# Four operand buffers for the heads of sequences 0 and 1; the last eight weight slots and the output operands change place

## The chip, the core and the metric

The kernel runs on one core of a Trainium2 chip. The metric is the device time of one execution in microseconds (us). Times below are medians of several executions; the views of the profile come from one execution that was taken by the hardware profiler.

TensorE (PE) does the matmuls, with its weight loads (PEld) beside them; VectorE (DVE), ScalarE (ACT) and GpSimd (POOL) do elementwise work; SyncE's queue (SP) starts the transfers (DMA). Each works through its own instructions in program order, and waits where an operand or a buffer is not yet there.

## What is computed

Retention attention with a fixed decay per head, then two feed-forward layers, all in 32-bit floats:

```python
gamma = 1.0 - 2.0 ** (-5.0 - np.arange(H))                   # B, H, S, D = 8, 8, 576, 64
Dmat = np.where(rel >= 0, gamma ** rel, 0.0)                 # rel = pos[:, None] - pos[None, :]
attn = np.matmul(scores * Dmat, v)                           # scores = q k^T / 8
x = attn.transpose(0, 2, 1, 3).reshape(4608, 512)
h = np.maximum(np.maximum(x @ w1, x @ w2), x @ w3)           # 512 -> 768
x = h @ w_out                                                # 768 -> 512
h = x @ w_in                                                 # 512 -> 2048
out = (h * np.clip(h + 3.0, 0.0, 6.0) / 6.0) @ w_out         # 2048 -> 512
```

## The kernel before

**The work and its pieces.** A unit is one pair of heads of one sequence: four units for each of the eight sequences, numbered 0 to 31. Its operands (queries, keys and values of both heads in several layouts) fill one buffer of 128 partitions x 3392 floats, which two transfers of 560 KB load (`load_raw`, L221 from `in_hi` and L224 from `in_lo`), after POOL has zeroed two corners of it (L217, L218). Sequences 0 and 1 (units 0 to 7, class `Summed`) are done at the start by a quicker route than the rest:

- `prepare`: eight multiplications of the keys on ACT (L364);
- `keys_mm`: 16 score matmuls (L268) and 16 wide matmuls (L374) on PE, where each of the wide ones needs one of the eight multiplications;
- `keys_rest`: mask (L289) and growth factors (L386) on DVE;
- `values_mm`: the ninth chunk's scores (L268) and 16 value matmuls (L310) on PE;
- `values_rest`, `last_mm`, `last_rest`: one more mask (L289) and the decay (L314) on DVE, the two last value matmuls on PE, the split of the result into a high and a low part (L55 on ACT, L56 on DVE) for `x`, the operand of the first layer, and for `xe`, which keeps the 64 tokens left over of each sequence. `xe` has one buffer; a transfer (`xed`, L355) empties it after each sequence.

**What runs between the units.** From unit 4 on, two blocks of the first layer follow each unit (`block`, 12 matmuls each of 128x512, L438 to L440; the eight blocks of `early`). The weights of that layer come as 64-bit words, 24 tiles in all. `wa.step` turns one tile at a time into two 32-bit parts: two integer operations on DVE (L116, L117), two on ACT (L119, L122), two more on DVE (L127, L129), one on POOL (L131); then a cast on ACT (L109) and the low part on POOL (L135). A step also starts the load of another tile (`ws`, L97, three buffers). A block's result is copied by ACT (L453) or joined by DVE (L455), and every third one is split into `h` (L55, L56).

**Buffers of units 0 to 7.** Two buffers `raw` and, for units 2 and 3 alone, two buffers in the pool `rooms`. After unit 3 the pool is released, and the pool `moe` (`t`, `h`, `y` of the first layer) takes its place, each of its tiles waiting for what it overlays. Units 4 to 7 have the two `raw` buffers: units 4 and 5 are loaded when units 0 and 1 are done, unit 6 when unit 4 is done, unit 7 when unit 5 is done. Every engine's order is the order in which the program is written (a manual schedule). The loop over the units is, in short:

```python
            if i < HP and i + 2 < HP + 2:       # units 2 to 5
                us[i + 2].prepare()
                us[i + 2].keys_mm()
...
            if i >= HP:
                load_raw(i + 2)
                wa.step()
                flush()
                block(*early.pop(0))
                if i + 2 < len(us):             # units 6 and 7
                    us[i + 2].prepare()
                    us[i + 2].keys_mm()
```

So the keys of units 2 to 5 stand between the values and the last matmuls of the unit two before, those of units 6 and 7 behind its second block. `flush` issues the low parts and transfers that were put off (`late`).

**After the units.** The rest of sequences 0 and 1's first layer runs from a written plan, with weight steps between. Then each sequence's four units run between the blocks of the one before, and the second layer's weights are turned into their parts alongside. From about the middle of the span the second layer runs in 48 groups (6 parts of the tokens x 8) of 7 products of 128x384 each and the projections to the output; each group writes four split operands by `gated` (L55, L56).

**The slots.** Of the 24 weight tiles the first 16 lie in slots `w`, the last 8 in slots `v`, both in the pool `w_pool`. When the first layer is done, the `w` slots take the output weights, and the eight `v` slots (128 x 1024 floats each) take `gated`'s operands and the output rows of `store`.

## Time and profile before

| | |
|---|---|
| time, median of 3 executions | 1555.34 us (1551.84 to 1555.36) |
| time of the profiled execution | 1550.61 us |
| its span, first to last instruction | 1548.8 us |
| TensorE busy | 1491.1 us, 96% of the span |
| VectorE busy | 903.1 us, 58% |
| ScalarE, GpSimd busy | 445.7 us, 29%; 175.6 us, 11% |
| mean granted TensorE clock | 0.989 of full speed |

The profiled execution took 4.7 us less than the median of the others. Its busy times add up over stages with different limits, so the table only says where to look: TensorE is idle for 58 us in all, and the question is in which stage, and on whom it waits there.

### The profile page before, as it was taken

The numbers are of one execution on the slowest core, as the hardware profiler recorded it, in microseconds if no ns is written. First come the engines' busy times: TensorE is split into PE (matmuls) and PEld (weight loads), VectorE is DVE, ScalarE is ACT, GpSimd is POOL, SyncE is SP. The second block draws the span as 40 slices with busy tenths as digits, with TensorE's granted clock in tenths as the row PEclk, the third lists the DMA queues.
The fourth block names the chain that finished last, engine by engine and source line by source line (L and its number), as shares of the span: only waits on it lengthen the run. The fifth ranks groups of instructions, "written<-read, shape, count | busy, mean of one in ns | idle before, by whom it ended". The sixth has DMA issues, their size and how long they took to land.

```text
span 1548.8 us, 24614 instructions
## 1 busy us (share of the span) xinstructions
PE 1491.1 (96%) x9664; PEld 1261.8 (81%) x9664; DVE 903.1 (58%) x1951; ACT 445.7 (29%) x878; POOL 175.6 (11%) x196
## 2 busy tenths in 40 slices
PE   6779999999999999799999999999999999999998
PEld 4557877888888888688888889888898888888887
DVE  4777666867676767512444655655655556565453
ACT  3434322332333233311222222222222223223221
POOL 1335400222222222300000000000000000000000
PEclk9989999999999999899999999999999999999999
DMA  9544135556565655405464435426336445444431
GB/s 217 143 124 124 67 88 136 152 170 173 186 157 167 181 183 145 177 41 197 136 218 116 121 128 184 118 88 226 115 89 230 118 115 196 121 114 132 146 102 41
DMA packets 94659, 220.01 MB, mean 142 GB/s; under 512 B 18320, under 2 KB 21648, under 8 KB 90448
## 3 DMA queue, kind: packets, MB, share of 16 engines
q1 hardware_dynamic: 94544, 218.44, 47.5%
q8 instruction: 77, 1.26, 0.3%
q14 instruction: 38, 0.31, 0.1%
HBM read 174.36 MB, written 44.04 MB: 141 GB/s over the span
## 4 chain that ended last, share of the span: by engine, by line
PE 52%; DVE 4%; ACT 1%; issue 0%; ACTq 0%
PE mm L438 9%; PE mm L440 9%; PE mm L439 9%; PE o L730 5%; PE o L731 5%; PE o L729 5%; PE p L730 2%; PE p L729 2%; PE p L731 2%; DVE g L688 1%; PE o L438 1%; PE o L440 1%; PE o L439 1%; DVE v L56 1%; DVE cc L695 1%; DVE g L687 1%
## 5 line engine op out<-in xcount | busy, mean ns | idle before, releaser
L55 ACT CAST v<-g 128x384 fp32r<-128x384 f32 x192 | 98.6, 513 | 364.5 <-DVE g L688 354.2
L438 PE MATMUL mm<-x,w 128*128 128x512 f32 x468 | 189.2, 404 | 11.7 <-ACT t L453 11.4
L695 DVE TENSOR_TENSOR cc<-mm,c 128x384 f32<-128x384 f32 x144 | 79.8, 554 | 197.0 <-ACT c L700 187.4
L439 PE MATMUL mm<-x,w 128*128 128x512 f32 x468 | 184.8, 395 | 0.0
L440 PE MATMUL mm<-x,w 128*128 128x512 f32 x468 | 184.3, 394 | 0.0
L56 DVE TENSOR_TENSOR v<-g,v 128x384 fp32r<-128x384 f32 x192 | 107.3, 559 | 112.3 <-ACT v L55 111.7
L455 DVE TENSOR_TENSOR t<-mm,t 128x512 f32<-128x512 f32 x108 | 74.3, 688 | 156.4 <-PE mm L440 150.4
L730 PE MATMUL o<-w,v 128*128 128x512 f32 x384 | 151.1, 393 | 0.0
L731 PE MATMUL o<-w,v 128*128 128x512 f32 x384 | 151.0, 393 | 0.0
L729 PE MATMUL o<-w,v 128*128 128x512 f32 x384 | 150.6, 392 | 0.0
L438 PE MATMUL mm<-T,wq 128*128 128x384 f32 x384 | 130.6, 340 | 2.5 <-ACT c L700 1.6
L440 PE MATMUL mm<-T,wq 128*128 128x384 f32 x384 | 129.5, 337 | 0.0
L439 PE MATMUL mm<-T,wq 128*128 128x384 f32 x384 | 129.2, 337 | 0.0
L700 ACT COPY c<-mm 128x384 f32<-128x384 f32 x144 | 68.7, 477 | 178.4 <-PE mm L440 178.4
L131 POOL TENSOR_TENSOR wf<-wf,wp 128x512 f32<-128x512 f32 x56 | 77.5, 1384 | 354.6 <-DVE wp L129 333.7
L438 PEld LDWEIGHTS mm<-x,w 128*128 128x128 f32 x468 | 89.0, 190 | 33.0 <-ACT t L453 12.2
L440 PEld LDWEIGHTS mm<-x,w 128*128 128x128 f32 x468 | 89.3, 191 | 19.3
L439 PEld LDWEIGHTS mm<-x,w 128*128 128x128 f32 x468 | 89.2, 191 | 17.4
L438 PE MATMUL mm<-B,wq 128*128 128x384 f32 x288 | 97.8, 340 | 2.1 <-DVE g L688 1.9
L440 PE MATMUL mm<-B,wq 128*128 128x384 f32 x288 | 97.0, 337 | 0.0
L439 PE MATMUL mm<-B,wq 128*128 128x384 f32 x288 | 96.9, 336 | 0.0
L289 DVE TENSOR_TENSOR raw<-at,mask_sb 64x256 f32<-64x256 f32 (+2 forms) x156 | 56.6, 363 | 54.9 <-PE at L268 35.6
(129 smaller groups left out, 2950.0 us busy)
## 6 DMA issues: line engine op xcount, KB each, us to landing
wq<-wqd SPq DMA_DIRECT2D x336, 256.0 KB, 2.8
ws<-in_w_b SPq DMA_DIRECT2D x32, 512.0 KB, 7.5
raw<-in_hi SPq DMA_DIRECT2D x29, 560.0 KB, 5.7
raw<-in_lo SPq DMA_DIRECT2D x29, 560.0 KB, 7.9
ws<-in_w_a SPq DMA_DIRECT2D x24, 512.0 KB, 3.6
wqd<-y SPq DMA_DIRECT2D x24, 512.0 KB, 2.8
x2d<-y SPq DMA_DIRECT2D x18, 512.0 KB, 3.5
wod<-y SPq DMA_DIRECT2D x16, 512.0 KB, 3.1
```

Source lines behind the costliest of these rows:

```text
L55: nc.scalar.copy(hi, full)
L56: late.append(lambda: (eng or nc.vector).tensor_tensor(out=lo, in0=full, in1=f32(hi), op=ALU.subtract))
L131: nc.gpsimd.tensor_tensor(out=frac, in0=frac, in1=f32(power), op=ALU.mult)
L438: nc.tensor.matmul(ps, lhsT=wh, rhs=xh, start=first, stop=False, skip_group_check=read)
L439: nc.tensor.matmul(ps, lhsT=wh, rhs=xl, start=False, stop=False, skip_group_check=read)
L440: nc.tensor.matmul(ps, lhsT=wl, rhs=xh, start=False, stop=last, skip_group_check=read)
L455: nc.vector.tensor_tensor(out=tmp[t, f], in0=ps, in1=tmp[t, f], op=ALU.max)
L695: nc.vector.tensor_tensor(out=c, in0=a, in1=b, op=ALU.add)
L700: nc.scalar.copy(c, ps)
L729: nc.tensor.matmul(outs[s], lhsT=gh, rhs=wo[f][:, 0, :], start=start, stop=False)
L730: nc.tensor.matmul(outs[s], lhsT=gh, rhs=wo[f][:, 1, :], start=False, stop=False)
L731: nc.tensor.matmul(outs[s], lhsT=gl, rhs=wo[f][:, 0, :], start=False, stop=stop)
```

## The change

- The pool `moe` is allocated first, at the bottom of what was shared space; `rooms` lies above it and lives until unit 7 is done. Its two buffers are of one kind (`room`) now and serve units 2 and 3 and then units 6 and 7.
- `load_raw(i + 4)` follows every unit i up to 5: a unit is loaded when the unit four before it is done. Units 8 and 9 (the first of sequence 2) go into the `raw` buffers of units 4 and 5.
- The keys of all units from 2 to 7 stand between the values and the last matmuls of the unit two before.
- The `flush` after unit 3 is gone; what was put off there is issued at unit 4, behind its first weight step.
- After unit 7 `rooms` is released, and the eight slots `v` are allocated in its place (pool `v_pool`).
- `gated`'s operands and `store`'s rows get eight buffers of their own, `gp`, 128 x 768 floats, in the pool `m2` of the second layer.

```diff
@@ -64,6 +64,7 @@
     wq_d = [dram.tile([P, 7, 2, 2 * P], F32, name=f"wqd{j}") for j in range(F2 // 2)]
     wo_d = [dram.tile([P, 2, 512], F32, name=f"wod{f}") for f in range(F2)]
 
+    moe = tc.alloc_tile_pool(name="moe", bufs=1)
     rooms = tc.alloc_tile_pool(name="rooms", bufs=1)
     at = tc.alloc_tile_pool(name="at", bufs=1, side="right")
     ps_mm = ctx.enter_context(tc.tile_pool(name="ps_mm", bufs=2, space=PSUM))
@@ -138,7 +139,7 @@
         return w_pool.tile([P, 2, 512], F32R, tag="w", bufs=F2, name="w")
 
     def v_tile():
-        return w_pool.tile([P, 2, 512], F32R, tag="v", bufs=NA - F2, name="v")
+        return v_pool.tile([P, 2, 512], F32R, tag="v", bufs=NA - F2, name="v")
 
     def pair():
         return moe.tile([P, 2, 512], F32R, tag="hy", bufs=7, name="y")
@@ -237,6 +238,9 @@
         upper(VS1, Z0)
         lower(KN, HI)
         lower(VS0, RAW)
+
+    def room():
+        return rooms.tile([P, RAW], F32, tag="room", bufs=2, name="room")
 
     def decay(i):
         if i < len(units):
@@ -492,8 +496,8 @@
         nc.sync.dma_start(out=mask_sb[:, 1:], in_=mask[:, 1:])
         nc.sync.dma_start(out=qdec_sb, in_=qdec)
         wa.fetch(1)
-        load_raw(2, rooms.tile([P, RAW], F32, name="room2"))
-        load_raw(3, rooms.tile([P, RAW], F32, name="room3"))
+        load_raw(2, room())
+        load_raw(3, room())
         nc.vector.memset(rebias, -896.0)
         nc.scalar.mul(rebias, rebias, 2.0 ** 23)
         xs[0], xs[1] = x_tile(), x_tile()
@@ -525,7 +529,7 @@
             flush()
             if i >= HP:
                 block(*early.pop(0))
-            if i < HP and i + 2 < HP + 2:
+            if i + 2 < len(us):
                 us[i + 2].prepare()
                 us[i + 2].keys_mm()
             u.values_rest()
@@ -533,21 +537,15 @@
             if i + 1 < len(us):
                 us[i + 1].keys_rest()
             u.last_rest()
-            if i < 2:
-                load_raw(i + HP)
+            if i < HP + 2:
+                load_raw(i + HP, room() if i in (2, 3) else None)
             if i >= HP:
-                load_raw(i + 2)
                 wa.step()
                 flush()
                 block(*early.pop(0))
-                if i + 2 < len(us):
-                    us[i + 2].prepare()
-                    us[i + 2].keys_mm()
-            if i == HP - 1:
-                flush()
-                rooms.release()
-                moe = tc.alloc_tile_pool(name="moe", bufs=1, reuse_waits="tile")
         flush()
+        rooms.release()
+        v_pool = tc.alloc_tile_pool(name="v", bufs=1, reuse_waits="tile")
 
 
         plan = [(1, 0, j) for j in range(3)] + [(0, 0), (0, 2, 2)] + [(1, 1, j) for j in range(3)] + [(0, 1)]
@@ -681,12 +679,15 @@
         flush()
         todo = []
 
+        def g_tile():
+            return m2.tile([P, 2, TH], F32R, tag="gp", bufs=8, name="gp")
+
         def gated(full, s0, f):
 
             g = m2.tile([P, TH], F32, tag="g", bufs=2, name="g")
             nc.vector.tensor_scalar(out=g, in0=full, scalar1=3.0, scalar2=0.0, op0=ALU.add, op1=ALU.max)
             nc.vector.scalar_tensor_tensor(out=g, in0=g, scalar=6.0, in1=full, op0=ALU.min, op1=ALU.mult)
-            parts = v_tile()[:, :, :TH]
+            parts = g_tile()
             split(g, parts[:, 0], parts[:, 1])
             return [(s0 + s, parts[:, :, s * P:(s + 1) * P], f) for s in range(TH // P)]
 
@@ -708,7 +709,7 @@
             return [(slice(C * i, C * (i + 1)), out[(2 * s + i) * S + TB:(2 * s + i + 1) * S, :]) for i in range(2)]
 
         def store(p, s, ps):
-            ob = f32(v_tile()).rearrange("p a n -> p (a n)")[:, :DM]
+            ob = f32(g_tile()).rearrange("p a n -> p (a n)")[:, :DM]
             if s % 2:
                 nc.vector.tensor_scalar(out=ob, in0=ps, scalar1=1.0 / 6.0, scalar2=None, op0=ALU.mult)
             else:
@@ -752,6 +753,7 @@
                 times(Y, 1, "B21", True, True)
                 down(TT - 1, F1 - 1)
                 flush()
+                v_pool.release()
                 moe.release()
                 x_pool.release()
                 m2 = ctx.enter_context(tc.tile_pool(name="m2", bufs=1, reuse_waits="tile"))
```

Line numbers of the kernel after the change are up to 4 higher. Three places in the orders of the engines, before and after.

TensorE, unit 6's keys, before: the end of unit 4's second block (its last matmul stands first), then the keys of unit 6 (`raw`), then unit 5's ninth scores and its values.

```order
L440 MATMUL mm<-x,w 128x512
L268 MATMUL o_166<-raw 64x64 x16
L374 MATMUL o_167<-raw 64x512 x2
L374 MATMUL o_167<-raw 64x448 x2
L374 MATMUL o_167<-raw 64x384 x2
L374 MATMUL o_167<-raw 64x320 x2
L374 MATMUL o_167<-raw 64x256 x2
L374 MATMUL o_167<-raw 64x192 x2
L374 MATMUL o_167<-raw 64x128 x2
L374 MATMUL o_167<-raw 64x64 x2
L268 MATMUL o_164<-raw 64x64 x2
L310 MATMUL o_165<-raw 64x64 x16
```

After the change: the end of unit 4's first block, then the keys of unit 6 (now in `room`), then the two last value matmuls of unit 4.

```order
L444 MATMUL mm<-x,w 128x512
L272 MATMUL o_169<-room 64x64 x16
L378 MATMUL o_170<-room 64x512 x2
L378 MATMUL o_170<-room 64x448 x2
L378 MATMUL o_170<-room 64x384 x2
L378 MATMUL o_170<-room 64x320 x2
L378 MATMUL o_170<-room 64x256 x2
L378 MATMUL o_170<-room 64x192 x2
L378 MATMUL o_170<-room 64x128 x2
L378 MATMUL o_170<-room 64x64 x2
L314 MATMUL at_123<-raw 64x64 x2
```

The 32 matmuls moved ahead of unit 4's last matmuls and of one block. Unit 7's moved in the same way, from behind unit 5's second block to behind its first.

ScalarE at the same place, before: the copy of unit 4's first block, the split of unit 3's or 4's results (`x`, `xe`), a weight step, the eight multiplications for unit 6, and the next weight step's cast.

```order
L453 COPY t<-mm 128x512
L55 CAST x<-yr 128x512
L55 CAST xe<-yr 128x64
L109 CAST w<-wf 128x512
L119 ACTIVATE wp<-wp,rebias 128x512
L122 ACTIVATE wf<-wf 128x512
L364 ACTIVATE raw<-raw,kdec_sb 128x64 x8
L109 CAST w<-wf 128x512
```

After:

```order
L457 COPY t<-mm 128x512
L368 ACTIVATE room<-room,kdec_sb 128x64 x8
L55 CAST x<-yr 128x512
L55 CAST xe<-yr 128x64
L110 CAST w<-wf 128x512
L120 ACTIVATE wp<-wp,rebias 128x512
L123 ACTIVATE wf<-wf 128x512
L110 CAST w<-wf 128x512
```

The eight multiplications moved from behind a split and a weight step to right behind the copy. Unit 7's moved in the same way and now stand right behind the cast of the first `h`.

SyncE's queue from the load of unit 5 on, before (`xed` is the store of sequence 0's `xe`, the pair of `raw` behind it is unit 6, the next pair unit 7, the last row unit 8).

```order
L221 DMA raw<-in_hi 64x2240
L224 DMA raw<-in_lo 64x2240
L97 DMA ws<-in_w_a 128x512 x2
L355 DMA xed<-xe 1024x1x64
L97 DMA ws<-in_w_a 128x512
L221 DMA raw<-in_hi 64x2240
L224 DMA raw<-in_lo 64x2240
L97 DMA ws<-in_w_a 128x512 x2
L221 DMA raw<-in_hi 64x2240
L224 DMA raw<-in_lo 64x2240
L97 DMA ws<-in_w_a 128x512 x2
L221 DMA raw<-in_hi 64x2240
```

After: the two pairs of `room` are units 6 and 7, the pairs of `raw` behind them units 8 and 9.

```order
L222 DMA raw<-in_hi 64x2240
L225 DMA raw<-in_lo 64x2240
L98 DMA ws<-in_w_a 128x512
L222 DMA room<-in_hi 64x2240
L225 DMA room<-in_lo 64x2240
L98 DMA ws<-in_w_a 128x512
L222 DMA room<-in_hi 64x2240
L225 DMA room<-in_lo 64x2240
L98 DMA ws<-in_w_a 128x512
L359 DMA xed<-xe 1024x1x64
L222 DMA raw<-in_hi 64x2240
L225 DMA raw<-in_lo 64x2240
```

Unit 6's load moved ahead of a weight load, `xed` and another weight load; unit 7's ahead of `xed` and three weight loads. Each pair still waits for POOL's two corner writes, and these for the last reader of the buffer's earlier unit.

## Rows read from the trace of the kernel before

**Rows 1.** The page: span, and busy time of each engine.

```profile
span 1548.8 us, 24614 instructions
...
PE 1491.1 (96%) x9664; PEld 1261.8 (81%) x9664; DVE 903.1 (58%) x1951; ACT 445.7 (29%) x878; POOL 175.6 (11%) x196
```

**Rows 2.** Stretches: length; busy PE, PEld, DVE, ACT, POOL; clock; DMA share; GB/s.

```profile
60.00:80.00 20.00, 13.19 (x122) 8.82 (x121) 8.95 (x16) 5.79 (x16) 5.82 (x7) 0.83 0.49 128
...
1000.00:1200.00 200.00, 199.59 (x989) 178.76 (x988) 111.08 (x209) 53.10 (x105) 0.00 (x0) 1.00 0.47 148
```

**Rows 3.** TensorE's timeline, units 4 to 7; idle time and its releaser in brackets.

```profile
65.81 0.47 PE L268 MATMUL o<-raw 64*64 64x64 f32 x2 [3.53 <-DMA raw<-in_hi]
...
68.94 1.65 PE L268 MATMUL o<-raw 64*64 64x64 f32 x25 [2.66 <-DMA raw<-in_lo]
...
75.25 1.15 PE L310 MATMUL o<-raw 128*64 128x64 f32 x32
...
80.64 0.34 PE L310 MATMUL o<-raw 128*64 128x64 f32 x4 [1.27 <-DVE raw L289]
...
86.76 0.47 PE L268 MATMUL at<-raw 64*64 64x64 f32 x2 [2.82 <-DMA raw<-in_hi]
...
89.50 1.65 PE L268 MATMUL at<-raw 64*64 64x64 f32 x25 [2.27 <-DMA raw<-in_lo]
...
101.22 0.34 PE L310 MATMUL o<-raw 128*64 128x64 f32 x4 [1.32 <-DVE raw L289]
...
112.68 0.34 PE L310 MATMUL at<-raw 128*64 128x64 f32 x4 [3.71 <-DVE raw L289]
```

**Rows 4.** The same timeline, the keys of unit 3.

```profile
32.35 1.15 PE L268 MATMUL mm<-room 64*64 64x64 f32 x32
...
33.58 4.10 PE L374 MATMUL mm<-room 64*64 64x512 f32 x32
```

**Rows 5.** SyncE's queue: issue of transfers.

```profile
41.16 8.18 SPq L97 DMA_DIRECT2D ws<-in_w_a  x2
...
59.42 0.49 SPq L221 DMA_DIRECT2D raw<-in_hi  x1
...
59.96 0.59 SPq L224 DMA_DIRECT2D raw<-in_lo  x1
```

**Rows 6.** TensorE's timeline: last matmuls of units 2, 3 and 4.

```profile
45.52 0.34 PE L310 MATMUL o<-room 128*64 128x64 f32 x4
...
53.37 0.34 PE L310 MATMUL mm<-room 128*64 128x64 f32 x4
...
59.00 0.34 PE L310 MATMUL at<-raw 128*64 128x64 f32 x4
```

**Rows 7.** Transfers of the first 130 us: count, size, median us to landing.

```profile
room<-in_lo SPq DMA_DIRECT2D x2, 560.0 KB, 15.0
```

**Rows 8.** ScalarE's timeline: cast of the first h; keys of unit 7.

```profile
80.14 0.62 ACT L55 CAST h<-t 128x512 fp32r<-128x512 f32 x1 [7.50 <-DVE t L455]
...
89.54 2.03 ACT L364 ACTIVATE raw<-raw,kdec_sb 128x64 f32<-128x64 f32 x8 [2.84 <-DMA raw<-in_lo]
```

**Rows 9.** Unit 4's values to unit 7's last matmuls, columns as in rows 2.

```profile
54.97:112.68 57.71, 40.02 (x365) 28.27 (x365) 37.70 (x69) 21.27 (x49) 18.55 (x19) 0.88 0.49 120
```

**Rows 10.** VectorE's timeline: a block's joining, first operation of two weight steps.

```profile
61.69 0.41 DVE L116 TENSOR_SCALAR wp<-ws 128x512 uint32<-128x512 uint32 x1
...
79.41 0.69 DVE L455 TENSOR_TENSOR t<-mm,t 128x512 f32<-128x512 f32 x1 [11.00 <-PE mm L440]
...
88.52 1.47 DVE L116 TENSOR_SCALAR wp<-ws 128x512 uint32<-128x512 uint32 x1
```

**Rows 11.** VectorE's groups in the stretch of rows 9: count, busy us, mean ns.

```profile
L116 DVE TENSOR_SCALAR wp<-ws 128x512 uint32<-128x512 uint32 x7 | 4.9, 704 | 0.0
```

**Rows 12.** TensorE's timeline behind the units.

```profile
149.33 0.50 PE L438 MATMUL mm<-x,w 128*128 128x512 f32 x1 [1.87 <-ACT t L453]
```

**Rows 13.** The page's groups: the cast of the second layer's operands.

```profile
L55 ACT CAST v<-g 128x384 fp32r<-128x384 f32 x192 | 98.6, 513 | 364.5 <-DVE g L688 354.2
```

## The prediction

> **What bounds the kernel now.** I read the page first: TensorE is busy for 1491.1 us of the 1548.8 us span [rows 1], so 58 us are to be had from its waits and nothing from a faster side engine elsewhere. Then the stretches: from 1000 to 1200 us TensorE is busy for 199.59 of 200 us, from 60 to 80 us for 13.19 of 20 at a granted clock of 0.83 [rows 2]. So I went to TensorE's own timeline of the units, and there read what ended each pause. From unit 4's values to unit 7's last matmuls the stretch lasts 57.71 us, of which TensorE works 40.02 [rows 9]. Seven pauses make up nearly all of the rest [rows 3]: four in which the keys of unit 6 (3.53 and 2.66 us) and of unit 7 (2.82 and 2.27 us) wait for the two halves of their operands, and three in which the last value matmuls of units 5, 6 and 7 (1.27, 1.32, 3.71 us) wait for VectorE's mask. The reader should see two things: the transfers are late because they are issued late (unit 6's at 59.42 and 59.96, just behind unit 4's last matmuls at 59.00 [rows 5, 6]), not because the queue is full; and behind each load pause the clock has fallen.
>
> **What the change removes.** First, the four load waits: 3.53 + 2.66 + 2.82 + 2.27 = 11.28 us, if the loads are there in time. Unit 6's operands now go into unit 2's buffer. Its last matmuls end at 45.52 + 0.34 = 45.9 us [rows 6]; POOL's corner writes and the issue take some 0.5 us, so the two halves start at about 46.4 and 46.9. The weight load ahead of them in the queue went out at 41.16, the one now behind them at 49.0 (the last of the two that the row merges [rows 5]), so the queue stands still for nothing. Unit 6's halves took 65.81 - 59.42 = 6.4 us and 68.94 - 59.96 = 9.0 us from issue to the matmul that they released [rows 3, 5]. That puts the later half at about 55.9. The keys come right behind unit 4's first block, at 59.0 [rows 6]: 3 us to spare. Unit 7's buffer is free at 53.7 [rows 6], its halves are there by 63 at the same 9 us, and its keys cannot come before those of unit 6 end at 64.3, with two blocks still between: no wait.
>
> Second, the cold clock. From the second pause on, unit 6's keys take 75.25 - 68.94 = 6.31 us and unit 7's begin with the same row of 1.65 us, so I take as much for them [rows 3]; the same 32 matmuls of unit 3, at full clock, take 33.58 + 4.10 - 32.35 = 5.33 us [rows 4], or 5.2 without the two that ran before the second pause. That is 1.1 us each, 2.2 together, and goes with the waits, since TensorE would now come to these keys from an unbroken block.
>
> Third, 1.27 us before unit 5's last matmuls. They will stand behind unit 7's keys, 5.3 us of work that VectorE can use to finish its mask. This work hides it; without unit 7's keys there the 1.27 us would be back.
>
> Removed in all: 11.28 + 2.2 + 1.27 = 14.75 us.
>
> **What it adds.** No instruction is added but for order. (a) Unit 7's eight multiplications now stand behind ScalarE's cast of the first `h`, and that waits for VectorE's joining of the block which TensorE has just finished. Before, joining plus cast took from 79.41 to 80.76 [rows 8, 10], and the first multiplication of eight takes 2.03 / 8 = 0.25 us [rows 8]: 1.6 us after the block the first wide matmul may start, while the 16 score matmuls ahead of it cover only 1.15 [rows 4]. A pause of 0.5 us if VectorE is free at the block's end. VectorE is then in its second weight step of the pair; by its backlog up to 0.7 us more. I take 0.8, with 0.4 and 1.2 as ends. Unit 6's multiplications stand behind a mere copy, 0.6 us, under the scores: nothing. (b) Unit 4's last matmuls now come one key block later. VectorE waits there for TensorE, and its order goes on with the mask of the next unit only afterwards; since VectorE is busy for 37.70 of 57.71 us [rows 9], it has 20 us of idle time in this stretch, of which 14 go. Some 6 us remain, so VectorE nearly becomes the bound, and the waits of 1.32 and 3.71 us, which are VectorE's own backlog, stay as they are. (c) The store of sequence 0's `xe` goes out later by one weight step's four VectorE operations; the cast of unit 4's `xe` needs it, and comes later itself by a whole key block, 5.3 us: hidden. (d) The block of memory now called `gp` has as many buffers as `v` had, and the same order of casts; the first layer's last weights wait for units 6 and 7, done long before. Nothing, hidden by ScalarE's 364.5 us of idle time before these casts [rows 13].
>
> Sum: 14.75 - 0.8 = 14 us, with ends of 13.5 and 14.4 by (a) alone. VectorE's backlog at the third wait may be up to 1.2 us more or less, so 12 to 16 us. From the profiled 1550.6 us this gives 1536.6; the executions of the median lie 4.7 us higher, so I forecast **1541 us**, and 1539 to 1543 for this case. What follows the units keeps its order and starts, as before, from the point at which TensorE waits for VectorE; the later pause of 1.87 us at 149.33 [rows 12] moves with it.
>
> **Rivals.** (1) VectorE takes over as the bound. The first operation of a weight step took 0.41 us at 61.69 and 1.47 at 88.52 [rows 10], the longer one beside a POOL operation; the seven of the stretch come to 4.9 us [rows 11]. In a denser stretch more of them could fall on POOL's work. If all did, 7 x 1.47 - 4.9 = 5.4 us more on VectorE, which with 6 us of idle time left and its waits for TensorE between would pass almost whole to the end: a gain of about 9, so 1546 us. For it speaks that VectorE is the releaser of three of the seven pauses; against it, that the steps keep their place behind POOL's work of the step before. The Trainium skill, "SBUF — State Buffer", section "Who interferes with whom", says that VectorE and GpSimd share a port pair under an exclusive lock, where the loser waits for the whole instruction; by that rule these operations are blocked, not slowed, and the case is this rival's.
>
> (2) Unit 6's load is late. The first two `room` loads took 15.0 us in the median [rows 7], in a full queue. Then the lower half would land at 61.9, TensorE would wait 2.9 us and lose 1.1 to the clock: a gain of 10, 1545 us. Against it: from 60 to 80 us the transfers' share is 0.49 [rows 2], and 46 to 55 us carries just one more weight load.
>
> (3) The change does not do what it says: POOL or the queue holds the new loads until the next weight step is done, and the keys wait as before in another place. Then only the 1.27 us and a part of the first pause go, within 4 us: 1552 us. Against it stand the queue's issue times above.
>
> (4) Slower. The second layer's operands lie in a new place. If ScalarE's casts into `gp` (513 ns each [rows 13]) or VectorE's low parts were slower there and TensorE waited for them, each of the 48 groups would have to lose more than 14 / 48 = 0.29 us to undo the gain, and 0.39 us to be slower by 0.3%: 1560 us. Against it: shapes, counts and order are the same, and TensorE's pauses there sum to 0.41 us in 200 [rows 2].
>
> **Chances.** Forecast (12 to 16 us): 0.60. VectorE as the bound: 0.17. Late load: 0.08. A larger gain, up to 20 us, where VectorE's backlog shrinks too: 0.03. No effect, or the gain lost later: 0.08. Slower: 0.04. A measurement of this kernel tells 0.3%, 4.7 us, from no change. So faster 0.88, same 0.08, slower 0.04. The range reaches from the larger gain to the two middle rivals with the executions' spread on top: 1536 to 1548 us.
>
> **What would show it.** Right: no pause of TensorE released by a transfer behind 30 us; keys of units 6 and 7 in 5.2 to 5.4 us each; a granted clock near 1 from 56 to 90 us; unit 6's two loads issued at 46 to 47 us; a pause before unit 7's wide matmuls of 0.4 to 1.2 us, released by ScalarE; waits of about 1.3 and 3.7 us for VectorE's mask before the last matmuls of units 6 and 7, and these last ones at about 98 to 99 us instead of 112.68. Wrong: a transfer still named there; unit 7's last matmuls earlier by 14 us but the end by less, which would put the loss behind the units; or TensorE's share in the second layer below that of before.

## The result, and the profile after

The kernel after the change takes 1538.56 us (median of 4 executions, 1535.74 to 1541.06), the kernel before, run beside it on the same chip, 1554.7 us. The ratio is 0.9899, 95% interval 0.9877 to 0.9921: faster by 16 us by the medians, with a forecast of 1541 and a range of 1536 to 1548. The profiled execution of after took 1537.66 us, 12.95 less than that of before. A later run of the same kernel gave 0.9912 [0.9899, 0.9925], 1538.31 us, 14.0 less than the kernel before beside it (1552.28).

The page after, span and busy times, beside [rows 1]:

```profile
span 1535.9 us, 24616 instructions
PE 1489.1 (97%) x9664; PEld 1260.6 (82%) x9664; DVE 904.3 (59%) x1951; ACT 445.9 (29%) x878; POOL 176.0 (11%) x196
```

TensorE's work is the same 9664 instructions. Of the 12.9 us by which the span is shorter, 10.9 are idle time of TensorE (57.7 us before, 46.8 after) and 2.0 are busy time. TensorE's timeline after, in the stretch of [rows 3] (start, length, the instruction, and in brackets idle time and its releaser; lines are up to 4 higher than before):

```profile
54.83 1.15 PE L314 MATMUL at<-raw 128*64 128x64 f32 x32 [1.00 <-DVE yr L318]
...
58.86 1.15 PE L272 MATMUL o<-room 64*64 64x64 f32 x32
...
63.88 0.34 PE L314 MATMUL at<-raw 128*64 128x64 f32 x4
...
71.40 1.15 PE L272 MATMUL at<-room 64*64 64x64 f32 x32
73.15 4.10 PE L378 MATMUL at<-room 64*64 64x512 f32 x32 [0.61 <-ACT room L368]
77.18 0.34 PE L314 MATMUL o<-raw 128*64 128x64 f32 x4
...
86.21 0.34 PE L314 MATMUL o<-room 128*64 128x64 f32 x4 [1.45 <-DVE room L293]
...
97.66 0.48 PE L314 MATMUL at<-room 128*64 128x64 f32 x4 [3.79 <-DVE room L293]
```

The reader should see what is gone from [rows 3]: no pause names a transfer any more, and unit 5's last matmuls (77.18) no longer wait. One pause is new, 0.61 us for ScalarE, and two waits for VectorE's mask are left as they were. Unit 7's last matmuls come at 97.66 us instead of 112.68.

SyncE's queue after, and the landing of unit 6's two halves (last number: median us from issue to landing):

```profile
45.87 0.47 SPq L222 DMA_DIRECT2D room<-in_hi  x1
46.38 0.59 SPq L225 DMA_DIRECT2D room<-in_lo  x1
48.87 0.33 SPq L98 DMA_DIRECT2D ws<-in_w_a  x1
...
58.55 0.60 SPq L359 DMA_DIRECT2D xed<-xe  x1
```

```profile
room<-in_hi SPq DMA_DIRECT2D x1, 560.0 KB, 5.5
room<-in_lo SPq DMA_DIRECT2D x1, 560.0 KB, 7.7
```

The later half is there at 46.38 + 7.7 = 54.1 us, 4.8 us before the keys that read it begin at 58.86. Before, the two halves went out at 59.42 and 59.96 [rows 5].

The stretch from unit 4's values to unit 7's last matmuls after, and the 16 us behind it (columns as in [rows 2]):

```profile
54.83:97.66 42.83, 36.96 (x364) 26.64 (x365) 38.98 (x69) 21.40 (x49) 18.98 (x17) 0.99 0.62 162
...
97.66:113.66 16.00, 16.00 (x61) 12.95 (x62) 9.83 (x16) 6.47 (x12) 6.47 (x6) 0.81 0.31 88
```

The same 16 us before:

```profile
112.68:128.68 16.00, 16.00 (x66) 13.08 (x67) 10.99 (x17) 6.79 (x13) 7.88 (x8) 0.89 0.72 186
```

57.71 us [rows 9] have become 42.83: 14.88 us gained where the change was made. Directly behind, TensorE gets through 61 matmuls in the 16 us in which it did 66 before, at a granted clock of 0.81 instead of 0.89. Unit 7's last matmuls and the four blocks behind them take 125.54 - 112.68 = 12.86 us before and 111.75 - 97.66 = 14.09 after: 1.2 us given back. From unit 7's last matmuls to the end of the span it is 1548.8 - 112.68 = 1436.1 us before, 1535.9 - 97.66 = 1438.2 after, and 1536.2 - 100.14 = 1436.1 in the second run of after. That run has the clock of 0.81 behind the units too, and is level with before at the end all the same. So the 1.2 us repeat, but that the whole time loses anything behind the units is not shown.

### The profile page after: what moved, and what is told of

It reads as the page before. It is cut to its first block, busy times and chain, and to the rows that moved or that the text cites. A ratio compares the mean times of both kernels' runs of the same rounds, so it can differ in the third digit from the quotient of the medians.

```text
span 1535.9 us, 24616 instructions
## 1 busy us (share of the span) xinstructions
PE 1489.1 (97%) x9664; PEld 1260.6 (82%) x9664; DVE 904.3 (59%) x1951; ACT 445.9 (29%) x878; POOL 176.0 (11%) x196
## 3 DMA queue, kind: packets, MB, share of 16 engines
q8 instruction: 77, 1.26, 0.3%
## 4 chain that ended last, share of the span: by engine, by line
PE 52%; DVE 4%; ACT 1%; issue 0%; ACTq 0%
PE mm L442 9%; PE mm L444 9%; PE mm L443 9%; PE o L731 5%; PE o L732 5%; PE o L730 5%; PE p L731 2%; PE p L730 2%; PE p L732 2%; DVE g L689 1%; PE o L442 1%; PE o L443 1%; PE o L444 1%; DVE cc L696 1%; DVE g L688 1%; ACT gp L55 1%
## 5 line engine op out<-in xcount | busy, mean ns | idle before, releaser
L55 ACT CAST gp<-g 128x384 fp32r<-128x384 f32 x192 | 98.5, 513 | 364.9 <-DVE g L689 356.2
L56 DVE TENSOR_TENSOR gp<-g,gp 128x384 fp32r<-128x384 f32 x192 | 107.2, 559 | 112.3 <-ACT gp L55 111.8
L731 PE MATMUL o<-w,gp 128*128 128x512 f32 x384 | 151.1, 393 | 0.0
L732 PE MATMUL o<-w,gp 128*128 128x512 f32 x384 | 151.0, 393 | 0.0
L730 PE MATMUL o<-w,gp 128*128 128x512 f32 x384 | 150.6, 392 | 0.0
L132 POOL TENSOR_TENSOR wf<-wf,wp 128x512 f32<-128x512 f32 x56 | 77.3, 1380 | 346.8 <-DVE wp L130 325.8
L293 DVE TENSOR_TENSOR raw<-at,mask_sb 64x64 f32<-64x64 f32 (+2 forms) x152 | 54.8, 361 | 55.6 <-PE at L272 35.4
```

Of the source, the lines that this page charges most:

```text
L55: nc.scalar.copy(hi, full)
L56: late.append(lambda: (eng or nc.vector).tensor_tensor(out=lo, in0=full, in1=f32(hi), op=ALU.subtract))
L132: nc.gpsimd.tensor_tensor(out=frac, in0=frac, in1=f32(power), op=ALU.mult)
L730: nc.tensor.matmul(outs[s], lhsT=gh, rhs=wo[f][:, 0, :], start=start, stop=False)
L731: nc.tensor.matmul(outs[s], lhsT=gh, rhs=wo[f][:, 1, :], start=False, stop=False)
L732: nc.tensor.matmul(outs[s], lhsT=gl, rhs=wo[f][:, 0, :], start=False, stop=stop)
```

## Experiments

For each kernel "stretch" is the time from unit 4's values to unit 7's last matmuls, the view that tells most: 57.71 us before, 42.83 after, and 42.84 (57.30 to 100.14) in the second run of after. The start of the stretch varies by some us, in part with the first loads, and from its end to that of the span the profiled executions below take 1435.3 to 1439.7 us, so whole times are worse evidence than the stretch. Ratios are to the kernel before, run beside on the same chip.

**1. After once more** (no edit).

> The changed kernel once more, on the same chip as the three kernels below, as their yardstick. Every theory: 12 to 17 us under the kernel before, ratio about 0.990; unit 7's last matmuls at 97 to 99 us.

0.9912 [0.9899, 0.9925], 1538.31 us, with the same stretch to 0.01 us: the measure by which the others are read.

**2. The loads alone.** After the change, but units 6 and 7's multiplications and keys back behind the second block:

```diff
-            if i + 2 < len(us):
+            if i < HP and i + 2 < HP + 2:
                 us[i + 2].prepare()
                 us[i + 2].keys_mm()
...
                 block(*early.pop(0))
+                if i + 2 < len(us):
+                    us[i + 2].prepare()
+                    us[i + 2].keys_mm()
```

> Four buffers and loads four units ahead as in the changed kernel, but the keys of units 6 and 7 back behind the second block of units 4 and 5. Theory (the early loads carry the gain, the new place of the keys about 1 us): no pause of TensorE released by a transfer after 30 us, unit 7's last matmuls at 97.5 to 99.5 us, ratio to before 0.989 to 0.992. Rival (the gain comes from the new order, which gives VectorE time for its masks): at least half of the 16 us is gone, ratio 0.995 or more.

0.9968 [0.9956, 0.9981], 1547.74 us; stretch 104.23 - 54.07 = 50.16. TensorE's pauses in the place of the load waits, and ScalarE at the first of them:

```profile
65.86 5.57 PE L378 MATMUL o<-room 64*64 64x512 f32 x26 [3.20 <-ACT room L368]
...
83.31 3.88 PE L378 MATMUL at<-room 64*64 64x512 f32 x26 [1.96 <-ACT room L368]
```

```profile
63.66 0.24 ACT L55 CAST xe<-yr 128x64 fp32r<-128x64 f32 x1 [4.04 <-DMA xed<-xe]
63.81 0.61 ACT L110 CAST w<-wf 128x512 fp32r<-128x512 f32 x1
64.33 0.72 ACT L120 ACTIVATE wp<-wp,rebias 128x512 int32<-128x512 int32 x1
64.95 0.61 ACT L123 ACTIVATE wf<-wf 128x512 f32<-128x512 uint32 x1
65.47 2.00 ACT L368 ACTIVATE room<-room,kdec_sb 128x64 f32<-128x64 f32 x8
```

My theory after the result was that the early loads carry nearly all of the gain and the order about 1 us. It fell: the loads alone give 7.55 of the 14.88 us. The rival's ratio came out, but not its reason: the waits for VectorE's mask are 1.33 and 3.75 us, as after the change. The profiled execution, 1544.32 us, is one of the two fastest of six; by the medians the loads alone give 1552.28 - 1547.74 = 4.5 of 14.0 us, so in other executions the stretch may have been longer. The operands are there, but the eight multiplications stand behind the cast of `xe`, which waits 4.04 us for the store that empties its one buffer, and behind a whole weight step. A wait for a transfer has become a wait for ScalarE.

**3. The order alone, the loads late.** After's order, with units 6 and 7 loaded in the course of units 4 and 5, behind the weight step:

```diff
+            if i in (HP, HP + 1):
+                load_raw(i + 2, room())
...
-            if i < HP + 2:
-                load_raw(i + HP, room() if i in (2, 3) else None)
+            if i < 2 or HP <= i < HP + 2:
+                load_raw(i + HP)
```

> The changed kernel's buffers and order of the keys, but the loads of units 6 and 7 issued in units 4 and 5, behind the first weight step and the store of xe, so at about 59 and 70 us and more. Theory: a late load costs TensorE one for one and the clock besides; unit 6's keys wait 6 to 10 us for the transfers with a clock drop behind it, unit 7's wait again; unit 7's last matmuls at 106 to 115 us, ratio 0.995 to 1.003. Rival (the order carries the gain): ratio stays at 0.990 to 0.992.

1.0043 [1.0031, 1.0056], 1559.37 us; stretch 119.56 - 55.89 = 63.67. TensorE:

```profile
65.99 0.47 PE L272 MATMUL o<-room 64*64 64x64 f32 x2 [6.01 <-DMA room<-in_hi]
...
89.75 0.44 PE L272 MATMUL at<-room 64*64 64x64 f32 x2 [6.95 <-DMA room<-in_hi]
```

Keys that stand earlier only wait longer: with 1.88 and 1.96 us for the second halves the four waits come to 16.80 us, against 11.28 before. It cost more than I had expected (unit 7's last matmuls by 115 us, ratio up to 1.003). Part of the loss is not the order's: these loads go out later than before's, unit 6's at 60.31 instead of 59.42 and unit 7's at 82.96 instead of 81.06, which may be up to 2.8 us of it. Neither half of the change does without the other: the loads alone gain 7.55 us of the stretch, the order with late loads loses 5.96, both gain 14.88.

**4. The memory alone.** Before, with only the pools `moe`, `rooms`, `v_pool` and the buffers `gp` of after:

```diff
+    moe = tc.alloc_tile_pool(name="moe", bufs=1)
...
-            parts = v_tile()[:, :, :TH]
+            parts = g_tile()
...
-                rooms.release()
-                moe = tc.alloc_tile_pool(name="moe", bufs=1, reuse_waits="tile")
         flush()
+        rooms.release()
+        v_pool = tc.alloc_tile_pool(name="v", bufs=1, reuse_waits="tile")
```

> The changed kernel's memory (moe below, rooms above until unit 7, weight slots in the rooms' place, buffers of their own for the second layer's operands), with the loads and the order of the kernel before: units 4 to 7 in the two raw buffers. Theory: no part of the gain, ratio 0.998 to 1.002, unit 7's last matmuls at 112 to 113.5 us. Rival (the new places of the tiles, or blocks that no longer wait for the rooms, carry some of it): ratio 0.997 or less.

1.0003 [0.9994, 1.0013], 1552.62 us: in the whole time the new places cost and give nothing. The stretch is 114.60 - 55.63 = 58.97, 1.26 us longer than before, and unit 7's last matmuls come later than the 113.5 us expected. Unit 6's halves landed 8.2 and 10.3 us after their issue instead of 6.3 and 8.9, and the four waits for transfers came to 12.74 us instead of 11.28. Whether the places have a part in that, one profiled execution of each does not tell; measured against this kernel the change gains 16.1 us of the stretch instead of 14.88.

**5. Only the multiplications moved.** After, with ScalarE's eight multiplications where the change puts them and the keys on TensorE back behind the second block:

```diff
                 us[i + 2].prepare()
-                us[i + 2].keys_mm()
+                if i + 2 < HP + 2:
+                    us[i + 2].keys_mm()
...
                 block(*early.pop(0))
+                if i + 2 < len(us):
+                    us[i + 2].keys_mm()
```

> Loads and ScalarE's multiplications for units 6 and 7 as in the changed kernel, their keys on TensorE behind the second block as in the kernel before. Theory (what the new order buys is ScalarE's multiplications, out of the queue behind a split and a weight step): no pause of ScalarE's before the wide matmuls of unit 6, the wait of about 1.3 us before unit 5's last matmuls back, from unit 4's values to unit 7's last matmuls 43 to 44.5 us, ratio to before 0.990 to 0.993. Rival (the keys' own place on TensorE is what counts): that stretch stays near the 50.2 us of the loads alone, ratio 0.996 to 0.998.

0.989 [0.9877, 0.9904], 1535.33 us; stretch 99.82 - 57.28 = 42.54, as after. TensorE has just three pauses there:

```profile
74.92 0.34 PE L314 MATMUL o<-raw 128*64 128x64 f32 x4 [1.27 <-DVE raw L293]
...
88.38 0.34 PE L314 MATMUL o<-room 128*64 128x64 f32 x4 [1.32 <-DVE room L293]
...
99.82 0.48 PE L314 MATMUL at<-room 128*64 128x64 f32 x4 [3.78 <-DVE room L293]
```

Unit 5's 1.27 us are back and the new 0.61 us are gone. The stretch is 7.62 us shorter than with the loads alone, a little better than expected. So what the order buys is ScalarE's place in its own queue; TensorE's keys could have stayed.

**6. Two buffers for `xe`, loads alone.** Experiment 2 with a second buffer, so that the cast of `xe` waits for no store:

```diff
-                xe[b] = at.tile([P, 2, KM, C], F32R, tag="xe", bufs=1, name="xe")
+                xe[b] = (rooms if b == 1 else at).tile([P, 2, KM, C], F32R, tag="xe", bufs=1, name="xe")
```

> The loads alone, with a second buffer for xe in free space beside the rooms, so that unit 4's cast of xe no longer waits for the store of sequence 0's. Theory (of ScalarE's two waits with the loads alone, the first, 3.2 us and a clock drop, comes from the store of xe that blocks the queue ahead of the multiplications, the second from their place alone): the first shrinks to 0.5 to 1.3 us, the second stays at about 2 us, from unit 4's values to unit 7's last matmuls 46.5 to 48 us instead of 50.2, ratio to before 0.994 to 0.9965. Rival (the place of the multiplications is all): 3 us or more as before, stretch 50 us.

0.9919 [0.9903, 0.9935], 1540.25 us; stretch 103.86 - 55.39 = 48.47. TensorE, and ScalarE's cast and multiplications:

```profile
65.50 3.88 PE L378 MATMUL o<-room 64*64 64x512 f32 x26 [1.52 <-ACT room L368]
...
81.25 5.57 PE L378 MATMUL at<-room 64*64 64x512 f32 x26 [1.96 <-ACT room L368]
```

```profile
63.30 0.24 ACT L55 CAST xe<-yr 128x64 fp32r<-128x64 f32 x1 [2.36 <-DVE yr L318]
...
65.11 2.00 ACT L368 ACTIVATE room<-room,kdec_sb 128x64 f32<-128x64 f32 x8
```

The cast now waits 2.36 us for VectorE where it waited 4.04 for the store. So the store takes 4.04 - 2.36 = 1.68 us, which is what the first pause lost (3.20 - 1.52), and the stretch is shorter by 1.69. That these agree so well is in part luck, for a slow spell of the clock moved as well: in either kernel one of the two groups of wide matmuls takes 5.57 us and the other 3.88, in experiment 2 unit 6's is the slow one and here unit 7's. The weight step ahead of the multiplications keeps the rest (1.52 here, and 1.96 before unit 7's in either kernel). The theory's direction came out; the first pause and the stretch are longer than it said (0.5 to 1.3 and 46.5 to 48 us), the ratio is lower.

The whole time fell by 7.5 us against experiment 2, the profiled executions by 1544.32 - 1540.95 = 3.4. Of the latter 3.4 - 1.7 = 1.7 us lie before and behind the stretch, and no view shows that the edit made them. In experiment 2 the time goes with the mean granted clock: 0.993 in the two executions of 1544.2 and 1544.3 us, 0.990 or 0.991 in the four of 1547.4 to 1550.1. Where the clock is lower in those four, and so why the medians stand further apart, stays open.

**7. Two buffers for `xe`, whole change.** The same edit on after.

> The changed kernel with the second buffer for xe. Theory (in the changed kernel the multiplications stand ahead of that cast, so ScalarE's 2.8 us of waiting for the store are hidden): the wait goes, the stretch stays within 0.4 us of 42.8, ratio 0.989 to 0.992. Rival (that wait delays the weight steps, and with them the last waits for VectorE): the stretch 1 to 3 us shorter, ratio 0.988 or less.

0.9902 [0.9884, 0.9919], 1538.14 us; stretch 99.75 - 56.91 = 42.84, as after to 0.01 us. ScalarE's cast of unit 4's `xe`, which after the change waits 2.82 us for the store, here waits 2.55 us for VectorE's `yr`: in this order the store adds just 0.27 us to a wait that is there anyhow, and no multiplication stands right behind the cast. Against experiment 6, on the same chip, the whole change is 5.63 us better in the stretch, but only 2.1 by the medians, with intervals that overlap. Once `xe` has two buffers, what the order adds is sure in the stretch alone.

**8. The low part of `xe` on GpSimd.** After, with VectorE's `xe` operation of units 0 to 7 given to POOL:

```diff
-            split(y[:, TB:], xe[b][:, 0, hp, :], xe[b][:, 1, hp, :])
+            split(y[:, TB:], xe[b][:, 0, hp, :], xe[b][:, 1, hp, :],
+                  nc.gpsimd if isinstance(self, Summed) else None)
```

> The changed kernel with the low part of xe of units 0 to 7 on GpSimd instead of VectorE (about 1.3 us of VectorE's time in each unit). Theory (VectorE's queue sets the two waits that are left): the waits of 1.45 and 3.8 us before the last matmuls of units 6 and 7 shrink to under 0.5 and to 2 to 3 us, unit 7's last matmuls 2 to 3.5 us earlier than in the changed kernel and the end 2 to 4 us earlier, ratio 0.987 to 0.990. Rival (GpSimd's own queue or the port that it shares gives it back): waits as before, ratio 0.991 or more.

0.9885 [0.9871, 0.9898], 1534.59 us; stretch 96.70 - 52.64 = 44.06, 1.2 us longer than after (ScalarE's cast of `xe` now waits 7.27 us for the store, and the pause for its multiplications grows from 0.61 to 1.67 us). TensorE's waits for VectorE stand as they were:

```profile
85.12 0.34 PE L314 MATMUL o<-room 128*64 128x64 f32 x4 [1.45 <-DVE room L293]
...
96.70 0.34 PE L314 MATMUL at<-room 128*64 128x64 f32 x4 [3.92 <-DVE room L293]
```

So the theory fell: the waits are those of its rival, though the ratio lies in the theory's range. What was won lies earlier: in this profile TensorE's pauses of 1.07, 1.00 and 1.00 us before the values of units 2, 3 and 4 are gone (the last of them is the first row of after's timeline). Another 2.1 us of the shorter span lie behind the stretch, where the two runs of after differ by as much.

**9. The low part of `xe` left out.** On experiment 7's kernel; the low part for sequences 0 and 1 is set to zero once each by POOL, so the 64 left-over tokens of both are computed from the high part alone:

```diff
+            if isinstance(self, Summed):
+                if hp == 0:
+                    nc.gpsimd.memset(f32(xe[b])[:, 1], 0.0)
+                nc.scalar.copy(xe[b][:, 0, hp, :], y[:, TB:])
+            else:
+                split(y[:, TB:], xe[b][:, 0, hp, :], xe[b][:, 1, hp, :])
```

> The changed kernel with the second buffer for xe, and the low part of xe of units 0 to 7 left out: GpSimd sets it to zero once for each sequence, so the output for those sequences' last 64 tokens is computed from the high part alone. It takes 1.3 us from VectorE in each unit and gives nothing to another engine. Theory (in units 4 to 7 the first operation of VectorE's that falls on GpSimd's work waits for it, whichever it is): the next one, of the weight step, grows from 0.4 to 1.4 us or more, the waits before the last matmuls of units 6 and 7 stay at 1.3 to 1.5 and 3.5 to 4 us, as with the low part on GpSimd. Rival (with the low part on GpSimd it was the added work there that gave the time back): these waits shrink to under 0.5 and to under 3 us.

0.988 [0.9857, 0.9903], 1534.88 us; stretch 96.82 - 54.10 = 42.72, as after. TensorE's waits:

```profile
85.36 0.34 PE L314 MATMUL o<-room 128*64 128x64 f32 x4 [1.33 <-DVE room L293]
...
96.82 0.48 PE L314 MATMUL at<-room 128*64 128x64 f32 x4 [3.77 <-DVE room L293]
```

VectorE and POOL ahead of the first of them, after the change:

```profile
80.21 1.75 DVE L56 TENSOR_TENSOR x<-yr,x 128x512 fp32r<-128x512 f32 x1
81.89 1.31 DVE L56 TENSOR_TENSOR xe<-yr,xe 128x64 fp32r<-128x64 f32 x1
83.13 0.41 DVE L117 TENSOR_SCALAR wp<-ws 128x512 uint32<-128x512 uint32 x1
...
85.70 0.46 DVE L293 TENSOR_TENSOR room<-o,mask_sb 64x64 f32<-64x64 f32 x2
```

```profile
79.83 1.59 POOL L132 TENSOR_TENSOR wf<-wf,wp 128x512 f32<-128x512 f32 x1 [1.62 <-DVE wp L130]
81.38 1.74 POOL L136 TENSOR_TENSOR w<-wf,w 128x512 fp32r<-128x512 f32 x1
```

The same place without the low part:

```profile
79.50 1.76 DVE L56 TENSOR_TENSOR x<-yr,x 128x512 fp32r<-128x512 f32 x1
81.18 1.51 DVE L117 TENSOR_SCALAR wp<-ws 128x512 uint32<-128x512 uint32 x1
...
84.85 0.46 DVE L293 TENSOR_TENSOR room<-o,mask_sb 64x64 f32<-64x64 f32 x2
```

```profile
79.12 1.59 POOL L132 TENSOR_TENSOR wf<-wf,wp 128x512 f32<-128x512 f32 x1 [1.62 <-DVE wp L130]
80.67 1.74 POOL L136 TENSOR_TENSOR w<-wf,w 128x512 fp32r<-128x512 f32 x1
```

Taking an operation of 1.31 us from VectorE made the next one 1.10 us longer. Most of the 1.31 us was waiting already: the shortest `xe` operation of the kernel before takes 0.21. In either kernel the operation that meets POOL's L136 ends just behind it: 81.89 + 1.31 = 83.20 against POOL's 81.38 + 1.74 = 83.12, and 81.18 + 1.51 = 82.69 against 80.67 + 1.74 = 82.41. What sets VectorE's time here is POOL's operation, and not the one on VectorE that waits for it. This is the rule of the Trainium skill, "SBUF — State Buffer", section "Who interferes with whom": whoever issues first has the shared ports for the whole instruction, and the other blocks. The traces agree, with these numbers.

The second wait stays by another route in part: without the low part VectorE's next L117 first waits 0.59 us for POOL's L132 (it starts at 92.68), and then takes 1.48 us, to just behind POOL's L136. And ahead of the values of units 2 to 4 the time did come free. There the next operation is the mask (L293), which takes 0.46 us beside POOL's L132 as it does elsewhere, and the three pauses that are gone in experiment 8 are gone here too.

**10. The mask first.** After, with `values_rest` of units 4 to 7 ahead of the weight step:

```diff
+            if i >= HP:
+                u.values_rest()
...
-            u.values_rest()
+            if i < HP:
+                u.values_rest()
```

> The changed kernel with the mask and decay of units 4 to 7 on VectorE ahead of the weight step instead of behind it. Both theories: the waits of 1.45 and 3.8 us go, unit 7's last matmuls 3 to 4.5 us earlier. Theory (behind the units the weight steps on VectorE and GpSimd set the pace, and these are no earlier): the three pauses behind the units, 3.5 us together in the changed kernel, grow by 2 to 3 us, and the end is only 0 to 2 us earlier, ratio 0.990 to 0.992. Rival (TensorE's own work sets the pace there): all of it comes through, ratio 0.987 to 0.989.

0.9918 [0.9904, 0.9931], 1540.1 us; stretch 99.84 - 58.67 = 41.17, 1.66 less than after, where I had expected 3 to 4.5. TensorE at its end and right behind:

```profile
99.84 0.34 PE L314 MATMUL at<-room 128*64 128x64 f32 x4 [0.83 <-DVE room L293]
...
107.88 0.50 PE L443 MATMUL mm<-x,w 128*128 128x512 f32 x1 [2.47 <-DVE x L56]
...
109.70 0.50 PE L442 MATMUL mm<-x,w 128*128 128x512 f32 x1 [1.09 <-DVE t L459]
```

Of the 1.45 + 3.79 us before the last matmuls of units 6 and 7 only 0.83 are left. But inside the stretch waits for VectorE of 0.76, 0.37 and 1.09 us are new and ScalarE's grows from 0.61 to 0.89, and 2.47 + 1.09 come back as waits for `x` and `t` behind the units: VectorE's debt is paid one step later, and the time as a whole is that of after, as the theory had it.

**11. Both VectorE edits** (8 and 10 together).

> The two edits before this together: the low part of xe on GpSimd, and mask and decay ahead of the weight step. Theory: the weight steps come 2 to 3 us earlier by the first edit and TensorE by both, so the end is 2.5 to 5 us earlier than in the changed kernel, ratio 0.986 to 0.989. Rival (nothing left to gain here, what is won is given back behind the units): ratio 0.990 to 0.992.

0.9871 [0.9854, 0.9888], 1532.85 us, the lowest median of all; stretch 39.07:

```profile
52.09:91.16 39.07, 37.07 (x367) 26.55 (x364) 31.37 (x61) 19.47 (x46) 18.21 (x21) 1.00 0.75 182
```

VectorE's share falls from 38.98 of 42.83 us to 31.37 of 39.07, and with idle time of its own it pays less of the debt back (behind the units one wait of 2.56 us for `x` is left of the 2.47 + 1.09). The interval of the ratio lies below that of the second run of after and overlaps that of the first a little.

**12. All three edits** (8, 10 and the second `xe` buffer).

> The low part of xe on GpSimd, mask and decay ahead of the weight step, and the second buffer for xe. Theory: as the two together, 0 to 0.7 us better, ratio 0.985 to 0.989. Rival (in those two the store of xe held ScalarE by 3.9 us and cost time): 1.5 us or more better, ratio 0.984 to 0.9865.

0.9882 [0.9864, 0.9901], 1534.66 us, stretch 93.60 - 54.54 = 39.06: nothing on top of experiment 11, as experiment 7 would have it; the rival's 1.5 us or more did not come.

## Why the prediction was right

**The load waits (11.28 us), right.** All four are gone. Unit 6's halves went out at 45.87 and 46.38, forecast 46.4 and 46.9, and landed at 54.1, forecast 55.9. Rival 2, the late load, had taken the 15.0 us of a full queue [rows 7] for a queue that was not full. But experiment 2 shows a condition that the prediction did not price: with the multiplications in their old place 3.20 + 1.96 us of waits come back in the place of the four, released by ScalarE. The prediction looked at ScalarE only for the new order (a); that the new order was also what kept this wait away, it did not see.

**The cold clock (2.2 us), right in kind, too small.** TensorE's busy time in the stretch fell from 40.02 us [rows 9] to 36.96 for the same matmuls, 3.06 us. All of it lies in the two key blocks, as priced: the values' matmuls (L310, now L314) take 5.61 us in either kernel, and no line of the blocks differs by more than 0.04. The price was too small. Unit 6's keys took 63.88 - 58.86 = 5.02 us, where I had set 5.2 against 6.31, and the 0.47 us that the first keys of each block take before the second pause I had left out. In the stretch's row the granted clock went from 0.88 to 0.99.

**Unit 5's 1.27 us, right.** They are gone, and experiment 5, with unit 7's keys taken from there, has them back to the hundredth.

**(a) ScalarE's new wait (0.8 us, 0.4 to 1.2), right:** 0.61. VectorE was free at the block's end, so the 0.5 us without its backlog was the better figure. Experiment 5 shows that this and the 1.27 us are two sides of one move, worth 0.66 net at most; the two stretches are 0.3 us apart the other way.

**(b) VectorE's waits of 1.32 and 3.71 us stay, right:** 1.45 and 3.79. I expected 6 us of idle time to be left to VectorE; it has 42.83 - 38.98 = 3.85. From 77.57 to 85.70 the timeline shows it without a gap but for the time its operations stand behind POOL's. Rival 1 would have had the lengthened operations lie on the weight steps' first one; its group came to 3.9 us in after against 4.9 [rows 11], and the lock was met by `x` and `xe` instead (1.75 and 1.31 us; four of each come to 3.8 and 5.2 us, against 2.7 and 4.1 before). So VectorE's busy time rose by 1.3 us and not by 5.4, and its price was not due, but its mechanism is what keeps the first of these two waits and takes part in the second (experiment 9).

**(c) The store of `xe`, right in result, nearly so in "hidden".** ScalarE's cast of unit 4's `xe` did wait for it, 2.82 us:

```profile
64.79 0.24 ACT L55 CAST xe<-yr 128x64 fp32r<-128x64 f32 x1 [2.82 <-DMA xed<-xe]
```

The store went out at 58.55, and I had set the cast's delay against it without the store's own time. But the cast waits 2.55 us for VectorE without the store as well, so 0.27 us were not hidden, and nobody on TensorE waited for them (experiment 7). In the old order the store costs 1.7 us (experiment 6).

**(d) The memory, right in the whole time:** experiment 4. Rival 4 had no ground; TensorE is busy for 199.59 of 200 us from 1000 to 1200, as in [rows 2]. Rival 3 is answered by the queue.

**The sum.** In the stretch, by the rows: 11.28 + 1.27 + 3.06 - 0.61 - (1.45 - 1.32) - (3.79 - 3.71) = 14.79 us, against 14.88 measured and 14 forecast. What the prediction left out is the place behind the units: it said that what follows keeps its course, but behind the 3.79 us pause the clock stayed low for longer than before, 1.2 us in either run of after. In the profiled execution 2.1 us in all are lost behind the stretch, and it gained 12.95 us instead of 14; in the second run none are lost. So the stretch is where the prediction can be judged, and there it was 0.9 too low. Two signs it named were missed by little: unit 6's keys took less than 5.2 us, and unit 7's last matmuls came at 97.66 instead of 98 to 99. The rest of the distance, 1541 to 1538.56, is the 4.7 us that I added for the gap of the profiled execution to the median: for after that gap is 1538.56 - 1537.66 = 0.9. That the median came so near to the forecast is in part luck, since this gap and the loss behind the stretch work against each other.

## What to carry to other kernels

A load that is issued earlier is worth its wait only if every engine that handles the operand gets to it earlier too: follow the operand through each queue, and look at what stands ahead of its first reader there, waits of other buffers' stores included. An operation that is taken from VectorE beside a busy GpSimd may free nothing, where the next one stands in the same place behind the same lock; look at the end of GpSimd's operation first, and at which operation of VectorE's moves up. And measure such a change at the stretch that it touches: here the stretch after the change repeated to 0.01 us, while whole times moved by several. Where transfers set the waits, even the stretch does not repeat so well (57.71 us before, 58.97 in experiment 4).

## What was not expected of the hardware

- The eight multiplications' place on one engine, ScalarE, was worth as much of the stretch as both loads' earlier issue (7.6 of 14.9 us, experiments 2 and 5; 5.6 where `xe` has two buffers, experiments 6 and 7), though ScalarE works for only half of the stretch (21.40 of 42.83 us).
- An operation of 128x64 on VectorE took 1.31 us behind POOL's lock (0.21 at its shortest before), and one of 128x512 that took its place 1.51; clear of POOL the latter takes 0.41.
- After the same pause before unit 7's last matmuls (3.71 and 3.79 us) the granted clock over the next 16 us was 0.89 in the one kernel and 0.81 in the other, and 0.81 again in the second run of after. The length of the pause alone does not decide it: behind 3.92 us in experiment 8 it was 0.89. What does stays open.
